# One ring for K, V and the weights: K and V of two kv heads per transfer, wo behind V

## The chip, the core and the metric

The kernel runs on one core of a Trainium2 chip. The metric is the time of one execution on the device in microseconds (us); the kernel before has a median of 214.87 us in 3 runs (214.87 to 214.9). Inputs and outputs lie in HBM.

## What is computed

One decode step for 4 sequences of one token each, with attention over the last 2,048 positions of a cache beside an MLP of two layers. Cut to what matters:

```python
def _A_ref(x, k_cache, v_cache, wq, wo):         # x (4, 1, 576); caches (4, 16, 8192, 128)
    W = min(4096, max(256, Sk // 4))             # 2048
    q = (x @ wq).reshape(B, Sq, 32, 128).transpose(0, 2, 1, 3)
    k = jnp.repeat(k_cache[:, :, Sk - W:, :], 2, axis=1)
    v = jnp.repeat(v_cache[:, :, Sk - W:, :], 2, axis=1)
    p = softmax(jnp.einsum("bhqd,bhkd->bhqk", q, k) * (128 ** -0.5))
    o = jnp.einsum("bhqk,bhkd->bhqd", p, v)
    return o.transpose(0, 2, 1, 3).reshape(B, Sq, 4096) @ wo

def _B_ref(x, w1, w2, w3, w4):
    h = gelu(layernorm(x) @ w1)
    ...
    x1 = x + hs                                  # with one token, half of hs's input is zero
    return x1 + gelu(layernorm(x1) @ w3) @ w4    # w3 (576, 4608), w4 (4608, 576)

xn = layernorm(A_x)
out = A_x + _A_ref(xn, A_k_cache, A_v_cache, A_wq, A_wo) + _B_ref(xn, B_w1, B_w2, B_w3, B_w4)
```

Everything is bf16. K and V are 33.6 MB each, the weights together 21.4 MB; each byte is read once.

## The kernel before

**Order of work.** The author writes each engine's work as a list of operations with a key (lines 165 to 178). The list is sorted by key (line 577), and each engine runs its own in that order; an operation waits for the semaphores of those named in `waits` (line 593). All large transfers are issued by SP, one behind the other, into one queue: a transfer that has to wait for a buffer holds up those behind it in SP's list. PE's work on K and on V stands in two loops of NIT = 4 passes (lines 374 to 388 and 453 to 456), each pass of four kv heads; all else is unrolled.

**Transfers.** SP's list (lines 216 to 251) is: wq in two pieces of two rows per partition and a ragged part, w2, w1, w3 in two pieces and a ragged part, then K. A kv head of K, for all 4 sequences, is one transfer of 2,048 KB: partition 4i + b holds positions 64i to 64i + 63 of sequence b, one run of 16 KB (lines 231 to 233). K goes through a ring of NKS = 4 such slots of its own, V through another of NVS = 4. wq, w1 and w2 lie in V's ring before V, w3 in `regB`, which later holds the transposed K. V0 is issued after K8 (`V0_AFTER`), V1 to V3 after K15, then wo into K's ring (`WO_AFTER`), then V4 to V15, each when the PV of four heads before is done (line 241), and w4 in five pieces (`W4P`, line 248), each when the last PV over its place in V's ring is done.

**Head of the kernel.** Layer norms; q = xn @ wq (line 316); w2 and w1 (line 497); w3 as h2_0 to h2_4, 12 matmuls each (lines 518 to 533); gelu2 (line 535); zeroS, which clears the scores' PSUM banks (line 338).

**K.** For each group of 8 x 128 positions, T (line 352) is 8 transposes on PE with `perm_k` as the moving operand, into one of 4 PSUM buffers; the copy out of PSUM (lines 356 to 360) is done by ACT for groups 1, 4 and 7 of each 8 and by DVE for the others, into 16 places of `ktbuf`. SC (lines 362 to 372) makes one kv head's scores in 16 matmuls of 512 columns, four sequences side by side in four column groups of PE. It is issued two groups after the last group that it needs (line 385). POOL copies each head's queries into `Qs` (line 390).

**Softmax.** rmax over all scores (line 394), exp on ACT in four parts (line 399), a transpose of 32 x 32 blocks on DVE (line 402), a permutation matmul PTp (line 403) and a copy PTs out of PSUM (lines 407 and 410, two each on ACT and DVE). PTg (line 413) spreads a head's probabilities over 4 sequences with the mask `bmask`, zero where the partition holds another sequence.

**V.** PV (lines 445 to 456) is 64 matmuls per head with V as the stationary operand and 8 columns of PTg; DVE scales the result into `OTx` (line 457).

**Tail.** After the last PV: turn (line 472), ORT (line 478), AO = 64 matmuls with wo (lines 466 to 479), MO0 = w4's first piece in 28 matmuls of 288 columns over four column groups, a fold of the four sums into two (lines 546 to 556), and MO1 to MO4 for the other four pieces, 88 matmuls of 144 columns over two column groups (lines 558 to 570). Then DVE and ACT copy the sums out (lines 571 and 572), and two transfers store them.

Of the kernel before, what the change touches and what calls it, by code (L numbers as in the profile page):

```python
# [12 lines left out]
NKS = 4  # L13
NVS = 4
NPG = 4
NKT = 16
NTB = 4
NIT = 4
ACT_EVAC = (1, 4, 7)
WO_AFTER = 3  # L20
V0_AFTER = 8
# [17 lines left out]
def bass_parallel_sum__sliding_block_cached__mixer_s_mlp__decode_kernel(  # L39
# [9 lines left out]
    NT = W // 32  # L49
    UE = NT * 128  # L50
    NHB = 8 * G
# [10 lines left out]
    with ExitStack() as ctx:  # L62
# [10 lines left out]
        kring = kring_t[:].rearrange("p (s t d) -> p s t d", s=NKS, t=NT)  # L73
        vring = vring_t[:].rearrange("p (s t d) -> p s t d", s=NVS, t=NT)
        ktbuf = regB_t[:, 0:NKT * 1024].rearrange("p (s n) -> p s n", s=NKT)
        kttile = regB_t[:, 0:NKT * 1024].rearrange("p (t b i) -> p t b i", b=B, i=32)
        w3main = regB_t[:, 0:4 * F].rearrange("p (r n) -> p r n", r=4)
        w3rag = regB_t[:, 4 * F:W3E]
        wqmain = vring_t[:, 0:4 * Hq * Dh].rearrange("p (r n) -> p r n", r=4)
        wqrag = vring_t[:, 4 * Hq * Dh:4 * Hq * Dh + Hq * Dh // 2]  # L80
        wo_sb = kring_t[:, 0:32 * D].rearrange("p (r n) -> p r n", r=32)
        _o = 4 * Hq * Dh + Hq * Dh // 2
        w1p = vring_t[:, _o:_o + 9 * HALF]
        _o += 9 * HALF
        w2p = vring_t[:, _o:_o + 9 * HALF]
        _o += 9 * HALF
        WQ_SLOTS = -(-_o // UE)
        assert WQ_SLOTS < NVS

# [53 lines left out]
        OTps = lambda g: ps[:, 4 + g % 4, 0:8]  # L143
# [41 lines left out]
        KT = KV + G + 8.0  # L185
# [12 lines left out]
        P(lambda e: e.memset(Qs[:, 3], 0.0), sig=("qs", 3), key=-95.8)  # L198

        def first_counts(e):  # L200
            for k in range(NTB):
                e.sem_inc(S[("eb", 32 - NTB + k)], 1)
                e.sem_inc(S[("on", k)], 1)
        P(first_counts, key=-95.7)
        P(lambda e: e.tensor_copy(out=perm_k[:].rearrange("p (b i) -> p b i", b=B), in_=ident_bf[:].rearrange("p (i b) -> p b i", b=B)),
          waits=["ident_bf"], sig="perm_k", key=-95.5)
        P(lambda e: e.tensor_copy(out=perm_p[:].rearrange("p (i b) -> p i b", b=B), in_=ident_bf[:].rearrange("p (b i) -> p i b", b=B)),
          waits=["ident_bf"], sig="perm_p", key=-95)
# [22 lines left out]
        def kv_pairs(ring_t, slot, cache, g):  # L231
            return [(ring_t[:, slot * UE:(slot + 1) * UE],
                     cache[:, g, Sk - W:Sk, :].rearrange("b (i t) d -> i b (t d)", t=NT))]

        for g in range(G):
            ev_k.append(add_dma(kv_pairs(kring_t, g % NKS, A_k_cache, g), ("k", g % NKS),
                                [f"T{8 * (g - NKS) + 7}"] if g >= NKS else [], g))
        wo_wait = f"T{8 * (G - 2) + 7}"
        for g in range(G):
            kk = KS + g if g else V0_AFTER + 0.5  # L240
            w = [f"PV{g - NVS}"] if g >= NVS else (["hT"] if g < WQ_SLOTS else [])
            ev_v.append(add_dma(kv_pairs(vring_t, g % NVS, A_v_cache, g), ("v", g % NVS), w, kk))
            if g == WO_AFTER:
                ev_wo = add_dma([(kring_t[:, 0:32 * D], A_wo.rearrange("(p r) n -> p (r n)", r=32))],
                                "wo", [wo_wait], kk + 0.1)
        w4_src = B_w4.rearrange("(p r) n -> p r n", r=RT)
        w4_sb = vring_t[:, 0:RT * D].rearrange("p (t n) -> p t n", n=D)
        for n, (t0, t1_) in enumerate(W4P):
            lst = (t1_ * D - 1) // UE
            ev_w4.append(add_dma([(w4_sb[:, t0:t1_, :], w4_src[:, t0:t1_, :])], ("w4", n),  # L250
                                 [f"PV{max(g for g in range(G) if g % NVS == lst)}"], KS + G + 0.1 * n))
# [94 lines left out]
        def pe_T(n):  # L346
            g, k = n // 8, n % 8

            def f(e):
                ins = None  # L350
                for t in range(8):
                    ins = e.transpose(tb[n % NTB][:, t, :], kring[:, g % NKS, 8 * k + t, :], perm_k[:])  # L352
                return ins
            return f
# [7 lines left out]
        def pe_SC(g):  # L362
            def f(e):
                ins = None
                for c4 in range(4):
                    for b in range(B):
                        t0 = 8 * ((8 * g + 2 * c4) % NKT)
                        ins = e.matmul(Sps[32 * b:32 * b + 32, c4, :].rearrange("p (t i) -> p t i", t=16), lhsT=Qs[:, g % 4, b, :],  # L368
                                       rhs=kttile[:, t0:t0 + 16, b, :],
                                       start=False, stop=(g == G - 1), tile_position=(0, 32 * b), skip_group_check=True)  # L370
                return ins
            return f

        for n in range(NHB):
            p = n % 32
            w = [("L", ("k", p // 8), 16)] if p % 8 == 0 else []
            w.append(("L", ("eb", (p - NTB) % 32), 1))
            add("pe", pe_T(n), waits=w, sig=f"T{n}", key=n // 32 + 0.01 * p, loop=("k", n // 32))
            eng, f = evac(n)
            add(eng, f, waits=[f"T{n}"] + ([f"SC{n // 8 - 2}"] if n >= 8 else []), sig=("eb", p), key=n + 0.2)  # L380
        for g in range(-1, G):
            s_ = g % 4
            if g < G - 1:
                add("pe", pe_SC(g), waits=[("L", ("eb", 8 * s_ + 6), 1), ("L", ("eb", 8 * s_ + 7), 1), ("L", ("qs", s_), 1)], sig=f"SC{g}",
                    key=(g + 1) // 4 + 0.01 * (8 * ((g + 1) % 4) + 1) + 0.005, loop=("k", (g + 1) // 4))
            else:
                add("pe", pe_SC(g), waits=[("c", ("eb", 30), NIT + 1), ("c", ("eb", 31), NIT + 1), ("c", ("qs", 3), NIT + 1)],
                    sig=f"SC{g}", key=NIT + 0.5)
        for g in range(G):
            P(lambda e, g=g: e.tensor_copy(out=Qs[:, g % 4], in_=Qpad[:, g]), waits=(["qT"] if g == 0 else []) + ([f"SC{g - 4}"] if g >= 3 else []),  # L390
              sig=("qs", g % 4), key=8 * g)


        add("dve", lambda e: e.tensor_reduce(out=rmax[:], in_=Sps, axis=AX.XY, op=ALU.max), waits=[f"SC{G - 1}"], sig="rmax", key=KS)  # L394
        add("dve", lambda e: e.tensor_scalar(out=negb[:], in0=rmax[:], scalar1=-scale, scalar2=None, op0=ALU.mult),
            waits=["rmax"], sig="negb", key=KS + 0.05)
        for q in range(4):
# [5 lines left out]
            add("pe", lambda e, q=q, cs=cs: e.matmul(ps[:, q, :], lhsT=perm_p[:], rhs=PTb[:, cs], start=True, stop=True),  # L403
                waits=[f"PTb{q}"] + (["perm_p"] if q == 0 else []), sig=f"PTp{q}", key=KS + 0.2 + 0.01 * q)
            dst = PTs[:, 16 * q:16 * q + 16, :].rearrange("p t r -> p (t r)")
            if q % 2 == 1:
                add("act", lambda e, q=q, dst=dst: e.activation(out=dst, in_=ps[:, q, :], func=ACTF.Copy), waits=[f"PTp{q}"],
                    sig=f"PTs{q}", key=KS + 0.3 + 0.01 * q)
            else:
                add("dve", lambda e, q=q, dst=dst: e.tensor_copy(out=dst, in_=ps[:, q, :]), waits=[f"PTp{q}"],  # L410
                    sig=f"PTs{q}", key=KS + 0.3 + 0.01 * q)
        for g in range(G):
            add("dve", lambda e, g=g: e.tensor_tensor(  # L413
                out=PTg[:, g % NPG], in0=PTs[:, :, 2 * g:2 * g + 2].unsqueeze(2).to_broadcast([128, NT, B, 2]),
                in1=bmask[:].unsqueeze(1).to_broadcast([128, NT, B, 2]), op=ALU.mult),
                waits=[f"PTs{q}" for q in range(4)] + ["bmask"] if g < NPG else [f"PV{g - NPG}"], sig=("pg", g % NPG),
                key=KS + 0.4 + 0.01 * g if g < NPG else KV + g - NPG + 0.6)
# [241 lines left out]
```

## Time and profile before

| what | value |
|---|---|
| median of 3 runs | 214.87 us |
| the profiled execution | 214.88 us |
| its span, first to last instruction | 213.6 us |
| HBM read in the span | 88.49 MB, 414 GB/s |
| mean granted TensorE clock | 0.776 |
| 16 K transfers, 2,048 KB each | 15.7 us from issue to landing (median) |
| 16 V transfers, 2,048 KB each | 17.6 us |
| wo, 4,608 KB | 23.6 us |

The prediction shows lines of the profile. In the page, the first part has each engine's busy time, its share of the span and its instructions; PE is the matmuls, PEld the loads of the stationary operand. The second part cuts the span into 40 slices of 5.3 us; a digit is the busy share in tenths, for PEclk the granted clock of TensorE in tenths, for DMA the busy share of the 16 DMA engines. The time from issue to landing holds the wait behind earlier transfers in the queue. In the timeline, a row is start, duration, engine, line, operation, output<-input, shapes and count, and in brackets the idle time before it with what ended it.

### The profile page before, as it was taken

The page shows a single profiled execution, that of the slowest core. Times are in us where ns is not written, and L with a number is a line of the kernel's source. Part 1 is how long each engine was busy: PE and PEld are TensorE (multiplying, and loading weights), DVE is VectorE, ACT ScalarE, POOL GpSimd, SP SyncE. Part 2 cuts the span into 40 slices and gives each one's busy share as a digit, 9 for nine tenths or more (in the row PEclk, how much of TensorE's full clock was granted, in tenths as well). Part 3 has the DMA queues.
Part 4 walks back from the last instruction along what each step waited for, and adds up shares of the span by engine and source line. Part 5 has one row for each costly group of instructions (what it writes and reads, how often), then busy time and mean ns, then how long its engine had stood idle before and what let it go on. Part 6 is the DMA issues. An engine that isn't in the chain of part 4 may idle for free.

```text
span 213.6 us, 5830 instructions
## 1 busy us (share of the span) xinstructions
PE 138.9 (65%) x2692; PEld 108.9 (51%) x2692; DVE 87.3 (41%) x162; ACT 59.3 (28%) x72; POOL 12.0 (6%) x39
## 2 busy tenths in 40 slices
PE   0089347999999994999999729823343443333585
PEld 0036123777777883788887503823343443333444
DVE  6725202566666664366666569611111112100000
ACT  2000302466665553266566654000000000000000
POOL 8501000000000100000000000000000000000000
PEclk9999855899999999699999995555555555555579
DMA  6999999999999999999999999999999999999993
GB/s 243 426 404 446 438 412 439 423 422 417 436 426 420 426 439 429 417 433 431 429 417 439 429 429 441 427 417 426 420 433 433 426 420 436 433 417 429 432 408 125
DMA packets 6657, 88.63 MB, mean 415 GB/s; under 512 B 748, under 2 KB 888, under 8 KB 1656
## 3 DMA queue, kind: packets, MB, share of 16 engines
q1 hardware_dynamic: 6632, 88.50, 97.8%
q8 instruction: 7, 0.11, 0.2%
q14 instruction: 2, 0.02, 0.0%
q10 hardware_dynamic: 16, 0.01, 0.0%
HBM read 88.49 MB, written 0.00 MB: 414 GB/s over the span
## 4 chain that ended last, share of the span: by engine, by line
DMA 52%; PE 39%; DVE 4%; issue 2%; SPq 1%; ACT 1%
PE ps L352 23%; DMA vring<-in_A_v_cache_dram 23%; DMA regB<-in_B_w_dram 12%; DMA kring<-in_A_k_cache_dram 8%; DMA vring<-in_B_w_dram 8%; PE ps L368 7%; PE ps L449 4%; PE ps L544 1%; PE ps L528 1%; DVE PTb L402 1%; SPq L176 1%; DVE rmax L394 1%; PE ps L341 1%; DVE regB L360 1%; ACT PTb L538 1%
## 5 line engine op out<-in xcount | busy, mean ns | idle before, releaser
L360 DVE COPY regB<-ps 128x1024 bf16<-128x1024 bf16 x80 | 52.4, 687 | 34.1 <-PE ps L352 32.3
L352 PEld LDWEIGHTS ps<-perm_k,kring 128*128 128x128 bf16 x1024 | 59.2, 100 | 11.6 <-issue 8.2
L352 PE MATMUL ps<-perm_k,kring 128*128 128x128 bf16 x1024 | 62.4, 222 | 3.2 <-DMA kring<-in_A_k_cache_dram 3.1
L359 ACT ACTIVATE regB<-ps 128x1024 bf16<-128x1024 bf16 x48 | 47.7, 1023 | 40.9 <-PE ps L352 40.9
L449 PE MATMUL ps<-PTg,vring 128*128 128x8 bf16 x1024 | 29.5, 168 | 39.0 <-DMA vring<-in_A_v_cache_dram 36.4
L449 PEld LDWEIGHTS ps<-PTg,vring 128*128 128x128 bf16 x1024 | 28.4, 104 | 40.1 <-DMA vring<-in_A_v_cache_dram 27.5
L457 DVE TENSOR_TENSOR PTb<-ps,PTb 128x32 bf16<-128x32 f32 x16 | 3.1, 192 | 56.1 <-PE ps L449 56.1
L368 PE MATMUL ps<-regB,Qs 128*32 128x512 bf16 x272 | 18.7, 396 | 4.6 <-issue 3.5
L554 ACT ACTIVATE P_sb<-ps 100x288 f32<-100x288 f32 x1 | 0.4, 411 | 75.8 <-PE ps L464 75.8
L368 PEld LDWEIGHTS ps<-regB,Qs 128*32 128x32 bf16 x272 | 6.6, 97 | 10.8 <-issue 6.4
L413 DVE TENSOR_TENSOR PTg<-PTs,bmask 128x512 bf16<-128x512 bf16 x16 | 10.7, 682 | 0.0
L390 POOL COPY Qs<-Qpad 128x128 bf16<-128x128 bf16 x16 | 4.6, 296 | 91.3 <-PE ps L368 82.0
L528 PE MATMUL ps<-regB,x1nT 128*32 128x432 bf16 (+1 forms) x60 | 4.4, 459 | 6.0 <-DMA regB<-in_B_w_dram 6.0
L541 DVE STREAM_TRANSPOSE h2T_sb<-PTb 128x1152 bf16<-128x1152 bf16 x1 | 1.4, 1379 | 11.4 <-ACT PTb L538 11.4
L528 PEld LDWEIGHTS ps<-regB,x1nT 128*32 128x32 bf16 x60 | 1.8, 122 | 8.0 <-DMA regB<-in_B_w_dram 6.6
L403 PE MATMUL ps<-PTb,perm_p 128*128 128x512 bf16 x4 | 2.4, 607 | 4.3 <-DVE PTb L402 4.1
L294 PE MATMUL ps<-ident_bf,xn_bf 4*128 4x4 bf16 x4 | 0.3, 166 | 7.5 <-DVE ragsrc L278 7.5
L571 DVE CAST out_sb<-ps 36x144 bf16<-36x144 f32 x1 | 0.3, 301 | 9.9 <-PE ps L544 9.9
L464 PE MATMUL ps<-kring,ORT 128*4 128x288 bf16 x64 | 4.0, 441 | 0.4 <-DVE ORT L478 0.4
L294 PEld LDWEIGHTS ps<-ident_bf,xn_bf 4*128 4x128 bf16 x4 | 0.2, 110 | 7.4 <-POOL ones_f L213 7.4
L316 PE MATMUL ps<-vring,xnT 128*32 128x512 bf16 x40 | 3.9, 571 | 0.0
L403 PEld LDWEIGHTS ps<-PTb,perm_p 128*128 128x128 bf16 x4 | 0.4, 104 | 6.3 <-DVE PTb L402 6.3
(99 smaller groups left out, 79.1 us busy)
## 6 DMA issues: line engine op xcount, KB each, us to landing
kring<-in_A_k_cache_dram SPq DMA_DIRECT2D x16, 2048.0 KB, 15.7
vring<-in_A_v_cache_dram SPq DMA_DIRECT2D x16, 2048.0 KB, 17.6
regB<-in_B_w_dram SPq DMA_DIRECT2D x2, 2304.0 KB, 23.5
kring<-in_A_wo_dram SPq DMA_DIRECT2D x1, 4608.0 KB, 23.6
vring<-in_A_wq_dram SPq DMA_DIRECT2D x2, 2048.0 KB, 9.6
vring<-in_B_w_dram SPq DMA_DIRECT2D x2, 2016.0 KB, 17.4
vring<-in_B_w_dram SPq DMA_DIRECT2D x2, 648.0 KB, 14.3
vring<-in_B_w_dram SPq DMA_DIRECT2D x1, 720.0 KB, 14.4
```

What stands on the lines that cost most here:

```text
L316: ins = e.matmul(Qps[32 * j:32 * j + 32, k, :], lhsT=x_, rhs=w, start=(r == 0), stop=(r == 4), tile_position=(0, 32 * j))
L352: ins = e.transpose(tb[n % NTB][:, t, :], kring[:, g % NKS, 8 * k + t, :], perm_k[:])
L359: return "act", lambda e: e.activation(out=ktbuf[:, n % NKT], in_=src, func=ACTF.Copy)
L360: return "dve", lambda e: e.tensor_copy(out=ktbuf[:, n % NKT], in_=src)
L368: ins = e.matmul(Sps[32 * b:32 * b + 32, c4, :].rearrange("p (t i) -> p t i", t=16), lhsT=Qs[:, g % 4, b, :], rhs=kttile[:, t0:t0 + 16, b, :],
L390: P(lambda e, g=g: e.tensor_copy(out=Qs[:, g % 4], in_=Qpad[:, g]), waits=(["qT"] if g == 0 else []) + ([f"SC{g - 4}"] if g >= 3 else []), ...
L403: add("pe", lambda e, q=q, cs=cs: e.matmul(ps[:, q, :], lhsT=perm_p[:], rhs=PTb[:, cs], start=True, stop=True), waits=[f"PTb{q}"] + (["per ...
L413: add("dve", lambda e, g=g: e.tensor_tensor(out=PTg[:, g % NPG], in0=PTs[:, :, 2 * g:2 * g + 2].unsqueeze(2).to_broadcast([128, NT, B, 2]) ...
L449: ins = e.matmul(OTps(g), lhsT=vring[:, g % NVS, t, :], rhs=PTg[:, g % NPG, t].rearrange("p b e -> p (b e)"), start=(t == 0), stop=(t == N ...
L457: add("dve", lambda e, g=g: e.tensor_tensor(out=OTx[:, :, 2 * g:2 * g + 2, :], in0=OTps(g).rearrange("p (b e) -> p b e", b=B).unsqueeze(3) ...
L464: return e.matmul(ACC[h], lhsT=lhsT, rhs=rhs, start=start, stop=stop, tile_position=(k0, 32 * h))
L528: ins = e.matmul(H2ps[k][32 * j:32 * j + 32, :], lhsT=x_, rhs=w, start=(r == 0), stop=(r == 4), tile_position=(0, 32 * j))
```

## The change

K and V are cut into 8 units of two kv heads (u and u + 8), 4,096 KB each; partition 8i + m holds positions 128i to 128i + 127 of the m-th of 8 pairs of sequence and head, one run of 32 KB. One ring of NSL = 4 such slots replaces both rings. The weights of the head lie in slots 1 to 3, so K0 goes to slot 0 at once, and K1 to K3 wait for h2_4, the last matmul with w3. w3 without its ragged part is one transfer. V0 to V3 each wait for the transposes of the unit of K that had the slot, V4 to V7 for the PV of four units before; wo waits for PV6 and stands behind V7, w4 behind wo without waits of its own. PE's loops have 2 passes, each of four units. SC is made in 32 pieces of 8 matmuls, each over four groups T. PTp has two permutations per part, so 8 matmuls and 8 copies PTs (4 on DVE, 4 on ACT). PTg is two operations per unit, each of 1,024 elements per partition, with a bf16 mask, in NPG = 2 buffers; PV is 128 matmuls of 16 columns per unit.

```diff
-NKS = 4
-NVS = 4
-NPG = 4
+NSL = 4
+NPG = 2
-NIT = 4
+NIT = 2
-WO_AFTER = 3
-V0_AFTER = 8
...
+    NU = G // 2
-    NT = W // 32
+    NT = W // 16
     UE = NT * 128
-    NHB = 8 * G
+    NB = NT // 8
+    NHB = NB * NU
...
-        kring_t = sb("kring", [128, NKS * UE], BF16)
-        vring_t = sb("vring", [128, NVS * UE], BF16)
-        W3E = 4 * F + FH
-        regB_t = sb("regB", [128, max(NKT * 1024, W3E)], BF16)
+        ring_t = sb("ring", [128, NSL * UE], BF16)
+        regB_t = sb("regB", [128, NKT * 1024], BF16)
...
-        for r in (0, 2):
-            ev_w3 += 2 * [add_dma([(w3main[:, r:r + 2, :], w3_src[:, r:r + 2, :])], ("w3", r), (), -12 + r)]
+        ev_w3 += 4 * [add_dma([(w3main, w3_src)], ("w3", 0), (), -12)]
...
+        def kv_pairs(slot, cache, u):
+            heads = cache.rearrange("b g s d -> (b g) s d")[u:B * G:NU, Sk - W:Sk, :]
+            return [(ring_t[:, slot * UE:(slot + 1) * UE], heads.rearrange("m (i t) d -> i m (t d)", t=NT))]
+
+        def k_done(u):
+            return f"T{NB * u + NB - 1}"
+        for u in range(NU):
+            w = [k_done(u - NSL)] if u >= NSL else (["h2_4"] if u else [])
+            ev_k.append(add_dma(kv_pairs(u % NSL, A_k_cache, u), ("k", u % NSL), w, u))
+        for u in range(NU):
+            w = [f"PV{u - NSL}"] if u >= NSL else [k_done(NU - NSL + u)]
+            ev_v.append(add_dma(kv_pairs(u % NSL, A_v_cache, u), ("v", u % NSL), w, KS + u))
+        ev_wo = add_dma([(wo_sb, A_wo.rearrange("(p r) n -> p r n", r=32))], "wo", [f"PV{NU - NSL + OUT_SLOT}"], KS + NU)
         w4_src = B_w4.rearrange("(p r) n -> p r n", r=RT)
         for n, (t0, t1_) in enumerate(W4P):
-            lst = (t1_ * D - 1) // UE
             ev_w4.append(add_dma([(w4_sb[:, t0:t1_, :], w4_src[:, t0:t1_, :])], ("w4", n),
-                                 [f"PV{max(g for g in range(G) if g % NVS == lst)}"], KS + G + 0.1 * n))
+                                 (), KS + NU + 0.1 * (n + 1)))
...
+        def pe_SC(c):
+            u, c4 = c // 4, c % 4
             def f(e):
                 ins = None
-                for c4 in range(4):
+                t0 = 8 * ((4 * c) % NKT)
+                for h in range(2):
                     for b in range(B):
-                        t0 = 8 * ((8 * g + 2 * c4) % NKT)
...
+                        ins = e.matmul(Sps[32 * b:32 * b + 32, c4, :].rearrange("p (t i) -> p t i", t=32), lhsT=Qs[:, 2 * (u % NSL) + h, b, :],
+                                       rhs=kttile[:, t0:t0 + 32, 2 * b + h, :],
+                                       start=False, stop=(u == NU - 1), tile_position=(0, 32 * b), skip_group_check=True)
...
+        for c in range(NHB // 4):
+            q = c % NQ
...
+            add("pe", pe_SC(c), waits=w, sig=f"SC{c}", key=c // NQ + 0.01 * (4 * q + 5) + 0.005, loop=("k", c // NQ))
...
+            def fan(e, j=j):
+                ins = None
+                for h in range(2):
+                    r = 2 * (j + NU * h)
+                    ins = e.tensor_tensor(out=PTg[:, j % NPG, :, :, 2 * h:2 * h + 2], in0=PTs[:, :, r:r + 2].unsqueeze(2).to_broadcast([128, NT, B, 2]),
+                                          in1=bmask[:, h].unsqueeze(1).to_broadcast([128, NT, B, 2]), op=ALU.mult)
+                return ins
...
                 for t in range(NT):
-                    ins = e.matmul(OTps(g), lhsT=vring[:, g % NVS, t, :], rhs=PTg[:, g % NPG, t].rearrange("p b e -> p (b e)"),
+                    ins = e.matmul(OTps(j), lhsT=ring[:, j % NSL, t, :], rhs=PTg[:, j % NPG, t].rearrange("p b e -> p (b e)"),
                                    start=(t == 0), stop=(t == NT - 1))
```

More of the change, by code (lines that the diff above doesn't have):

```diff
@@ L395, in bass_parallel_sum__sliding_block_cached__mixer_s_mlp__decode_kernel @@
+        for u in range(NU):
+            for h in range(2):
+                P(lambda e, u=u, h=h: e.tensor_copy(out=Qs[:, 2 * (u % NSL) + h], in_=Qpad[:, u + NU * h]),
+                  waits=(["qT"] if u + h == 0 else []) + ([f"SC{4 * (u - NSL) + 3}"] if u >= NSL else []),
+                  sig=("qs", 2 * (u % NSL) + h), key=u + 0.1 * h)
+        add("dve", lambda e: e.tensor_reduce(out=rmax[:], in_=Sps, axis=AX.XY, op=ALU.max), waits=[f"SC{NHB // 4 - 1}"], sig="rmax", key=KS)
         add("dve", lambda e: e.tensor_scalar(out=negb[:], in0=rmax[:], scalar1=-scale, scalar2=None, op0=ALU.mult),
```

188 lines of the change are left out of this document (89 added, 99 removed).

## Prediction

> **What bounds the kernel now.** I read the page first: the busy share of each engine, the DMA line in 40 slices, the clock line and the share of the DMA queue.
>
> ```profile
> PE 138.9 (65%) x2692; PEld 108.9 (51%) x2692; DVE 87.3 (41%) x162; ACT 59.3 (28%) x72; POOL 12.0 (6%) x39
> PEclk9999855899999999699999995555555555555579
> DMA  6999999999999999999999999999999999999993
> q1 hardware_dynamic: 6632, 88.50, 97.8%
> ```
>
> No engine is near its limit, and the transfers are: the queue that SP feeds takes 97.8% of 16 engines' span for 88.50 MB, and no slice but the first and the last is below 9. The change moves the same bytes. So the whole of its gain must lie in the rate while the queue is full, and it can lose in three ways: the queue runs dry, or the head or the tail grows, in which the queue is not the limit. For the rate I asked for windows in which runs of one size prevail (columns: stretch, length, busy time of PE, PEld, DVE, ACT, POOL, granted clock, DMA share, GB/s).
>
> ```profile
> 0.00:1.80 1.80, 0.00 (x0) 0.00 (x0) 0.00 (x0) 0.39 (x1) 1.13 (x8) 1.00 0.00 1
> 4.00:12.00 8.00, 1.04 (x20) 0.73 (x24) 6.10 (x18) 0.40 (x2) 4.08 (x13) 1.00 1.01 432
> 13.40:16.00 2.60, 2.17 (x28) 0.64 (x20) 0.38 (x1) 0.38 (x1) 0.00 (x0) 1.00 1.02 421
> 18.00:27.00 9.00, 5.24 (x60) 3.07 (x57) 3.49 (x11) 2.18 (x4) 0.42 (x2) 0.90 1.01 432
> 146.00:198.00 52.00, 19.81 (x684) 18.93 (x681) 6.89 (x19) 0.00 (x0) 0.00 (x0) 0.50 1.01 428
> ```
>
> wq in 16 KB runs goes at 432 GB/s, w2 and w1 in 5,184 B runs at 421, w3 in 18 KB runs at 432, V in 16 KB runs at 428. The end of the span I read from the chain (start, length, what) and from PE's timeline.
>
> ```profile
> 191.08 17.48 DMA vring<-in_B_w_dram
> 208.60 3.17 PE ps L544 x88
> 211.79 0.30 DVE out_sb L571
> ...
> 198.97 1.87 PE L449 MATMUL ps<-PTg,vring 128*128 128x8 bf16 x64 [3.03 <-DMA vring<-in_A_v_cache_dram]
> 201.97 4.01 PE L464 MATMUL ps<-kring,ORT 128*4 128x288 bf16 x64 [0.38 <-DVE ORT L478]
> 205.77 1.17 PE L464 MATMUL ps<-vring,h2T_sb 128*4 128x288 bf16 x28
> 207.46 0.66 PE L544 MATMUL ps<-P_sb,sel_h 100*4 100x144 f32 x8 [0.52 <-ACT P_sb L554]
> 208.60 3.15 PE L544 MATMUL ps<-vring,h2T_sb 128*4 128x144 bf16 x88 [0.48 <-DMA vring<-in_B_w_dram]
> ```
>
> The last V lands at 198.97 and its work ends at 200.84; AO (64 matmuls) follows at 201.97, MO0 (28) directly behind it, the fold, and at 208.60, when w4's second piece has landed, the 88 matmuls of MO1 to MO4. They follow w4's small pieces to the end.
>
> **The change, part by part.** The sum is made on the profiled execution, 214.88 us (span 213.6 and 1.3 around it); the median is 214.87, the same.
>
> *Longer runs.* 16 engines move a 16 KB run in 16 x 16,384 B / 432 GB/s = 607 ns each and a 5,184 B run in 16 x 5,184 / 421 = 197 ns: 410 ns for 11,200 B, which leaves 7 ns per run whatever its size. K and V are 4,096 runs now, 256 per engine; as 2,048 runs, 128 per engine are saved: 128 x 7 = 0.9 us. Bounds: w3's 18 KB runs are no faster than wq's 16 KB runs (both 432), so the gain may be 0.2; and if the two-head pattern brought K and V from 428 to wq's 432, 67.1 MB would save 1.5 us. I take 0.9, which is nearest to the rows of single sizes. Half as many K and V transfers and w3 in one are 17 transfers fewer in a queue that is never empty; nothing.
>
> *K1 behind h2_4.* Slots 1 to 3 hold the weights, so K1 to K3 wait on SP for the last matmul with w3, and V0 and all else queues behind them.
>
> ```profile
> 29.81 3.07 PE L528 MATMUL ps<-regB,x1nT 128*32 128x432 bf16 x36 [4.19 <-DMA regB<-in_B_w_dram]
> 34.24 1.89 PE L341 MATMUL ps<-zeros_bf 128*128 128x512 bf16 x4 [1.36 <-ACT PTb L538]
> 36.22 1.03 PE L352 MATMUL ps<-perm_k,kring 128*128 128x128 bf16 x8
> ```
>
> w3's second half lands at 29.8. In one transfer all of it lands then, and 60 matmuls instead of 36 follow: 3.07 x 60/36 = 5.1, so h2_4 ends at 34.9. From issue to first bytes it is 1.0 (SP's first issue stands at 0.80, and the window to 1.80 has no traffic): K1 moves from 35.9. The cover is K0 behind w3's ragged part, 4.78 MB at 428 = 11.2 us, to 41.0. Cost nothing, 5 us in hand; without K0 there it would cost those 6 us.
>
> *K on PE.* PE starts when all of K0 is there, 41.0 instead of 36.2.
>
> ```profile
> 44.43 3.71 PE ps L352 x64
> 48.13 0.24 issue
> 48.37 1.05 PE ps L368 x16
> ```
>
> A kv head takes 3.71 + 0.24 + 1.05 = 5.0 us: 64 transposes, a wait for the copy out of PSUM (SC follows the last copy that it needs by two groups, before and after) and 16 score matmuls. The change has the same matmuls, in SCs of 8, twice as often. So there is one more wait of up to 0.24 per head and one more start and drain of a group, which no row shows by itself: 0.1 to 0.5 more by an estimate from these rows; I take 0.35, the wait and 0.1: 5.35 per head, 10.7 per unit, against 9.8 for its transfer. Were 32 B pieces of the moving operand slower than 64 B ones, it would be more. K ends at 41.0 + 8 x 10.7 = 126.6, and up to 3.4 later, as PE waits for K0 from about 38 and may begin at half clock: about 128.5, rmax at 130 instead of 123.9.
>
> *V4 behind PV0* is what this delay can reach: one ring has V0 to V3 in its slots, and V4 may go when PV0 is done.
>
> ```profile
> 123.90 2.29 DVE L394 TENSOR_REDUCE rmax<-ps 128x1 f32<-128x2048 f32 x1 [1.82 <-PE ps L368]
> 129.87 1.25 DVE L410 CAST PTs<-ps 128x512 bf16<-128x512 f32 x2
> 131.62 2.49 DVE L413 TENSOR_TENSOR PTg<-PTs,bmask 128x512 bf16<-128x512 bf16 x4
> 132.36 3.80 PE L449 MATMUL ps<-PTg,vring 128*128 128x8 bf16 x136
> ```
>
> From rmax to the first PV matmul it is 8.5 us. Added: two casts more on DVE, 1.25, and a first PTg of two operations of 1,024 elements instead of one of 512 at 0.62: between 1.25 (bf16 mask, twice the rate) and 2.5, so 0.6 to 1.9 more. PV0 is 128 matmuls at 28 ns, 3.6. It ends at 130 + 8.5 + 1.9 to 3.1 + 3.6 = 144 to 145.2. The queue holds work until K0's 41.0 and eleven units of 9.8, less 0.7 of the gain: 148.1; V4 must be issued by 147. Cost nothing, with 2 to 3 us in hand, the thinnest cover. Later releases have more: wo waits for PV6, done 4 us after V6's landing, while V7 moves for 9.7.
>
> *wo behind V.* The bytes up to w4 are the same, so w4's second piece lands at 208.6 - 0.9 = 207.7. But AO now waits for wo instead of the last V. wo ends where the last V ended, at 198.97 - 0.9 = 198.1, V7's work being over by 193. AO runs 198.1 to 202.1; MO0 waits for w4's first piece, one 2,016 KB transfer (4.8 us) before the second, 202.9; the fold is done at 206; MO1 starts at 207.7. The chain AO, MO0, fold, which was one stretch, is now three with pauses. That bears on the clock:
>
> ```profile
> 120.00:124.00 4.00, 2.70 (x46) 1.86 (x43) 2.13 (x5) 3.32 (x3) 0.00 (x0) 1.00 1.03 438
> 124.00:128.00 4.00, 0.00 (x1) 0.01 (x1) 3.12 (x4) 1.59 (x6) 0.00 (x0) 0.94 1.01 429
> 128.00:132.00 4.00, 3.75 (x9) 0.75 (x10) 3.93 (x9) 2.40 (x6) 0.00 (x0) 0.50 1.06 459
> ...
> 202.65:206.05 3.40, 3.40 (x64) 2.01 (x60) 0.00 (x0) 0.00 (x0) 0.00 (x0) 0.50 0.98 417
> 206.05:208.60 2.55, 1.55 (x37) 0.73 (x29) 0.00 (x0) 0.41 (x1) 0.00 (x0) 1.00 0.97 395
> 208.60:211.75 3.15, 3.15 (x88) 2.61 (x88) 0.00 (x0) 0.00 (x0) 0.00 (x0) 1.00 0.44 167
> ```
>
> The granted clock is 0.50 through V, rose only at 206.05, after 4.1 us of unbroken matmuls, and had fallen by 128 after 4 us of idleness. Now AO alone is 4.0 us, then come 0.8 of idleness, MO0, the fold, 1.7 of idleness. I expect no rise that lasts to MO1. At full clock its matmuls take 144 columns in two column groups, 30 ns apiece (88 in 3.15 us with small waits); at half clock 60. 88 x 60 = 5.3 us from 207.7, and 0.2 for the last one to drain: 213.2 instead of 211.8. **+1.4 us**, the gain of 0.9 already in it.
>
> [...]
>
> Sum: 214.88 + 1.4 = 216.3 us.
>
> **The rivals.** *The tail keeps its clock* (faster). A rise within AO that outlives the two pauses: MO4 then ends behind w4's last bytes as now, and 0.9 is gained: 214.0. For it: AO is only 0.1 us shorter than the stretch that raised it. Against: the pauses, 2.5 us of six. With a gain of 0.2 it would be no change, 214.7. It decides from a clock of 1.00 at MO1's start.
>
> *V4 comes too late.* If K on PE is 3 us slower than reckoned (half clock at its start, more waits), the cover is used up, and every us beyond empties the queue and moves the tail: 1 to 3 us on top, 217.5 to 219.
>
> *PE's code is loaded again.* The K loop's body doubles, from 320 matmuls to 640 with their weight loads.
>
> ```profile
> 58.36 1.05 PE L368 MATMUL ps<-regB,Qs 128*32 128x512 bf16 x16 [0.27 <-issue]
> q8 instruction: 7, 0.11, 0.2%
> ```
>
> Now the second pass begins (about 58) with a pause of 0.27, like any other, so nothing is loaded again; seven fetches of 16 KB serve the whole run, each 0.002 x 16 x 213.6 / 7 = 1.0 us. If the longer body no longer stays, a fetch with its delay of 1.0 stalls PE about 2 to 3 us on the one return, all of the cover and perhaps 1 us more: 217.3. [...]
>
> *The change doesn't do what it says:* longer runs move at the old rate, gain 0.2, and the cold tail stands: 217.0.
>
> **How the numbers follow.** Chances: forecast 0.50 (its own range 215.4 to 216.9, from gains of 1.5 and 0.2), tail at full clock 0.20, V4 late 0.16, code 0.05, no faster runs 0.09. Likeliest: 216.3. The range takes in the full-clock tail at 214.0 and the late V4 to 218.6. A measurement here can tell about 0.2%, 0.43 us, from no change. Faster than that is the tail at full clock with most of the gain, 0.14; within it the same with little gain, or a gain of 1.5 with the clock rising midway, 0.11; slower the rest, 0.75.
>
> **What would show it.** Right: DMA share 9 in all slices; V at 430 to 431 GB/s; AO starting at about 198; a clock of 0.50 at MO1's start and some 5 us for the 88. Wrong: a clock of 1.00 there; a dip of DMA near 148 (V4) or 41 (K1); rmax later than 133; V at 428 or below, as then the two-head pattern costs rather than gains.

## The result and the profile after

The kernel after the change takes 376.56 us (median of 6 runs, 374.11 to 378.4), the kernel before 214.87 us in the runs beside it: a ratio of 1.752 (95% interval 1.744 to 1.759). The forecast of 216.3 us, its range and every rival are far off. The profiled execution took 377.55 us with a span of 376.3.

The page of the kernel after: the DMA lines of the 40 slices (9.4 us each now), then the share of the queue and the transfers of K and V.

```profile
DMA  8999999999999999999999999999999999999993
GB/s 323 446 404 256 223 195 197 224 214 218 202 211 219 218 219 216 219 220 216 216 212 216 216 214 212 214 212 211 202 218 216 212 206 206 216 212 214 412 420 132
...
q1 hardware_dynamic: 4184, 88.49, 97.9%
...
ring<-in_A_k_cache_dram SPq DMA_DIRECT2D x8, 4096.0 KB, 64.5
ring<-in_A_v_cache_dram SPq DMA_DIRECT2D x8, 4096.0 KB, 69.7
```

Read the DMA line alone, and nothing seems wrong: the engines are as busy as before, 97.9% for the same 88.49 MB. The line under it tells the story: K begins within the fourth slice (256 GB/s), and from the fifth to the last of V the same full engines move 195 to 224 GB/s; in the full slices of weights ahead of K and behind V they move 404 to 446. So no wait took the place of another. By these rates each packet takes twice as long (worked out below). The windows of the kernel after show that the rate belongs to K and V alone (columns as in the prediction):

```profile
4.00:12.00 8.00, 1.16 (x24) 0.83 (x28) 5.98 (x18) 0.41 (x2) 4.72 (x15) 1.00 1.01 430
...
60.00:180.00 120.00, 74.35 (x979) 57.11 (x979) 40.93 (x61) 37.09 (x37) 2.14 (x8) 0.76 1.00 215
210.00:340.00 130.00, 28.00 (x905) 25.18 (x903) 14.57 (x38) 1.22 (x3) 0.00 (x0) 0.50 1.00 211
360.00:365.00 5.00, 4.29 (x84) 2.46 (x80) 0.00 (x0) 0.00 (x0) 0.00 (x0) 0.65 1.00 423
```

V went at 428 GB/s before and goes at 211 now. With all 16 engines busy and 213 GB/s, between K's 215 and V's 211, a run of 32 KB takes 16 x 32,768 B / 213 GB/s = 2.46 us, where 1.22 would fit the rate before. A unit of 4,096 KB lands every 19.7 us instead of 2 x 4.9 = 9.8, and 16 x (19.7 - 9.8) = 158 us is nearly all of the 162 us by which the kernel is slower. The rest of the timeline of the kernel after, before K and after V, looks as it was forecast:

```profile
29.85 4.99 PE L548 MATMUL ps<-ring,x1nT 128*32 128x432 bf16 x60 [7.16 <-DMA ring<-in_B_w_dram]
34.88 1.82 SPq L180 DMA_DIRECT2D ring<-in_A_k_cache_dram  x3
...
359.58 4.01 PE L484 MATMUL ps<-ring,ORT 128*4 128x288 bf16 x64 [6.34 <-DMA ring<-in_A_wo_dram]
364.30 1.03 PE L484 MATMUL ps<-ring,h2T_sb 128*4 128x288 bf16 x28 [0.71 <-DMA ring<-in_B_w_dram]
...
369.44 4.98 PE L564 MATMUL ps<-ring,h2T_sb 128*4 128x144 bf16 x88 [2.93 <-DMA ring<-in_B_w_dram]
```

K1 is issued at 34.88; AO, MO0 and MO1 each wait for their weights with pauses between, and the 88 matmuls take 4.98 us.

### The profile page after: what moved, and what is told of

It reads as the page before. It is cut to its first block, busy times and chain, and to the rows that moved or that the text cites. A ratio compares the mean times of both kernels' runs of the same rounds, so it can differ in the third digit from the quotient of the medians.

```text
span 376.3 us, 5772 instructions
## 1 busy us (share of the span) xinstructions
PE 158.0 (42%) x2678; PEld 120.2 (32%) x2680; DVE 89.7 (24%) x164; ACT 61.0 (16%) x74; POOL 12.1 (3%) x41
## 3 DMA queue, kind: packets, MB, share of 16 engines
q1 hardware_dynamic: 4184, 88.49, 97.9%
HBM read 88.49 MB, written 0.00 MB: 235 GB/s over the span
## 4 chain that ended last, share of the span: by engine, by line
another core or an unknown queue 35%; PE 30%; DMA 27%; ACT 3%; DVE 3%; issue 1%; SPq 1%; DVEq 0%
DMA ring<-in_B_w_dram 17%; PE ps L356 16%; DMA ring<-in_A_k_cache_dram 10%; PE ps L464 7%; PE ps L374 5%; ACT regB L363 2%; PE ps L548 1%; PE ps L564 1%; SPq L180 1%; DVE PTb L408 1%; DVE PTs L419 1%; DVE rmax L400 1%; DVE PTg L426 0%; ACT P_sb L405 0%
## 5 line engine op out<-in xcount | busy, mean ns | idle before, releaser
L356 PE MATMUL ps<-perm_k,ring 128*128 128x128 bf16 x1024 | 77.2, 243 | 63.5 <-DMA ring<-in_A_k_cache_dram 63.5
L356 PEld LDWEIGHTS ps<-perm_k,ring 128*128 128x128 bf16 x1024 | 70.1, 111 | 81.1 <-DMA ring<-in_A_k_cache_dram 45.2
L464 PE MATMUL ps<-PTg,ring 128*128 128x16 bf16 x1024 | 28.6, 174 | 110.5 <-DMA ring<-in_A_v_cache_dram 110.1
L464 PEld LDWEIGHTS ps<-PTg,ring 128*128 128x128 bf16 x1024 | 27.9, 104 | 111.4 <-DMA ring<-in_A_v_cache_dram 94.2
L426 DVE TENSOR_TENSOR PTg<-PTs,bmask 128x1024 bf16<-128x1024 bf16 x16 | 10.2, 684 | 0.0
L548 PE MATMUL ps<-ring,x1nT 128*32 128x432 bf16 (+1 forms) x60 | 5.0, 525 | 7.2 <-DMA ring<-in_B_w_dram 7.2
L484 PE MATMUL ps<-ring,ORT 128*4 128x288 bf16 x64 | 4.0, 443 | 6.3 <-DMA ring<-in_A_wo_dram 6.3
L564 PE MATMUL ps<-ring,h2T_sb 128*4 128x144 bf16 x88 | 5.0, 307 | 2.9 <-DMA ring<-in_B_w_dram 2.9
L564 PEld LDWEIGHTS ps<-ring,h2T_sb 128*4 128x4 bf16 x88 | 4.8, 120 | 3.2 <-DMA ring<-in_B_w_dram 3.2
L320 PE MATMUL ps<-ring,xnT 128*32 128x512 bf16 x40 | 4.2, 607 | 0.0
```

The source lines that it names most:

```text
L320: ins = e.matmul(Qps[32 * j:32 * j + 32, k, :], lhsT=x_, rhs=w, start=(r == 0), stop=(r == 4), tile_position=(0, 32 * j))
L356: ins = e.transpose(tb[n % NTB][:, t, :], ring[:, u % NSL, 8 * k + t, :], perm_k[:])
L426: ins = e.tensor_tensor(out=PTg[:, j % NPG, :, :, 2 * h:2 * h + 2], in0=PTs[:, :, r:r + 2].unsqueeze(2).to_broadcast([128, NT, B, 2]), in1 ...
L464: ins = e.matmul(OTps(j), lhsT=ring[:, j % NSL, t, :], rhs=PTg[:, j % NPG, t].rearrange("p b e -> p (b e)"), start=(t == 0), stop=(t == NT ...
L484: return e.matmul(ACC[h], lhsT=lhsT, rhs=rhs, start=start, stop=stop, tile_position=(k0, 32 * h))
L548: ins = e.matmul(H2ps[k][32 * j:32 * j + 32, :], lhsT=x_, rhs=w, start=(r == 0), stop=(r == 4), tile_position=(0, 32 * j))
```

## The experiments

Three things are new in how K and V are read: the run is 32 KB, the eight pairs of one unit lie further apart in HBM than four sequences did, and the source's slowest dimension has 16 blocks (with 8 pairs each) where it had 32 (with 4 sequences each). **My theory after the result:** it is the split. By this theory a transfer is shared out over the 16 DMA engines by the slowest dimension, so that one engine gets whole blocks; the number of busy engines in e2 agrees (DMA share 0.50 with 8 blocks, 0.25 with 4, 0.13 with 2). With 16 x 8 each engine then has one block of 8 partitions, which I take to be 8e to 8e + 7 for engine e; with 32 x 4 it has two blocks of 4 partitions. Which engine has which block no trace here shows. Engines that run abreast may then hold each other up, depending on the partitions that they write; this was my estimate, and the runs below test it. **Rivals:** the distances in HBM; the length of the run.

**Transfers alone, one shape after the other (e1_streams).** A kernel without any computing reads eight streams of 16.8 MB. The shapes, as (count, stride) from slow to fast:

```python
("A", 8192, [(8192, 32), (16 * HEAD, 4)])      # 32 x 4, 16 KB runs: the kernel before
("B", RUN, [(RUN, 16), (8 * HEAD, 8)])         # 16 x 8, 32 KB runs: the kernel after
("C", 8192, [(RUN, 16), (8 * HEAD, 8)])        # 16 x 8, 16 KB runs
("D", RUN, [(RUN, 32), (16 * HEAD, 4)])        # 32 x 4, 32 KB runs
("E", RUN, [(RUN, 128)])                       # 128 x 1, contiguous
("G", RUN, [(RUN, 16), (HEAD, 8)])             # 16 x 8, pairs 2 MB apart
("H", RUN, [(RUN, 16), (16 * RUN, 8)])         # 16 x 8, contiguous
("I", RUN, [(RUN, 16), (8 * HEAD + 2048, 8)])  # 16 x 8, pairs 16 MB + 4 KB apart
```

> Only transfers, no arithmetic: the kernel leaves out the whole computation and stores zeros. Eight stages of 16.8 MB each, SP waiting for all transfers between them. A: the pattern of before (32 positions blocks x 4 sequences, 16 KB runs). B: the changed pattern (16 blocks x 8 heads that lie 16 MB apart, 32 KB runs). C: as B with 16 KB runs, twice as many transfers. D: 32 blocks x 4 sequences with 32 KB runs. E: 128 runs of 32 KB from one contiguous 4 MB. G: as B with 8 adjacent heads, 2 MB apart. H: 16 blocks x 8, but all from one contiguous 4 MB (8 parts 512 KB apart). I: as B with the heads 16 MB + 4 KB apart. All theories expect A at 428 GB/s (39 us) and B at 214 (78 us). Theory of the distance (streams that move at the same time read places a large power of two apart and share a part of HBM): C 214, D, E and H 428, I 428, G open. Rival, the run length (32 KB itself is slow): C 428, D, E, G, H and I 214. Rival, the split (a source of 16 x 8 runs is spread badly over the 16 engines): C, G, H and I 214, D and E 428.

The windows of this run, one in each stream (columns: stretch, length, busy time of DVE and POOL, granted clock, DMA share, GB/s):

```profile
3.00:40.00 37.00, 0.00 (x0) 0.00 (x0) 1.00 1.01 429
48.00:120.00 72.00, 0.00 (x0) 0.00 (x0) 1.00 1.01 211
130.00:200.00 70.00, 0.00 (x0) 0.00 (x0) 1.00 1.00 213
210.00:245.00 35.00, 0.00 (x0) 0.00 (x0) 1.00 0.98 425
252.00:287.00 35.00, 0.00 (x0) 0.00 (x0) 1.00 1.01 434
295.00:368.00 73.00, 0.00 (x0) 0.00 (x0) 1.00 1.00 208
378.00:450.00 72.00, 0.00 (x0) 0.00 (x0) 1.00 1.01 211
460.00:533.00 73.00, 0.00 (x0) 0.00 (x0) 1.00 1.00 208
```

A, D and E go at the full rate, the five streams of 16 x 8 at half of it. B and C differ in the run alone and are equal, as are A and D: run length falls. H reads one contiguous stretch and is as slow as B, and D, with sequences 32 MB apart, has the full rate: distance falls. What is common to the slow ones is 16 blocks of 8.

**How the rate falls with the split (e2_splits).** Again transfers alone, all contiguous, 32 KB runs: 64 x 2, 32 x 4, 16 x 8, 8 x 16, 4 x 32, 2 x 64 on 128 partitions, then two shapes on 64 partitions and one on 32, whose transfers go by turns to the lower and the upper half of SBUF.

```python
("8x16", RUN, [(2 * n * HEAD, [(RUN, 8), (8 * RUN, 16)]) for n in range(2)])
("64 of 64", 64, [(n * HEAD, [(RUN, 64)]) for n in range(4)])
("64 as 16x4", 64, [(n * HEAD, [(RUN, 16), (16 * RUN, 4)]) for n in range(4)])
```

> Only transfers, no arithmetic; zeros are stored. Nine stages, SP waiting between them, all from contiguous places, all in 32 KB runs, only the shape of the source differs: 128 partitions as 64x2 and 32x4 (four transfers of 4.2 MB each), 16x8 and 8x16 (two each), 4x32 and 2x64 (one each); then 64 partitions as 64 and as 16x4 and 32 partitions as 32, four transfers each, by turns in the lower and the upper half of SBUF. [...] Rival, the number of the slowest dimension alone (16 or fewer is slow for a reason on the side of the read): 64 partitions as 64 at 428, as 16x4 at 214.

Its windows, one per shape in that order (the last two columns are the ones to read):

```profile
1.00:39.00 38.00, 0.14 (x1) 0.00 (x0) 1.00 0.97 414
42.50:81.00 38.50, 0.00 (x0) 0.00 (x0) 1.00 0.98 420
84.50:124.00 39.50, 0.00 (x0) 0.00 (x0) 1.00 1.01 212
127.50:204.00 76.50, 0.00 (x0) 0.00 (x0) 1.00 0.50 110
207.00:283.00 76.00, 0.00 (x0) 0.00 (x0) 1.00 0.25 55
285.00:363.00 78.00, 0.00 (x0) 0.00 (x0) 1.00 0.13 54
365.00:405.00 40.00, 0.00 (x0) 0.00 (x0) 1.00 1.01 210
408.00:448.00 40.00, 0.00 (x0) 0.00 (x0) 1.00 0.99 210
450.50:471.00 20.50, 0.00 (x0) 0.00 (x0) 1.00 0.96 205
```

The DMA share counts engines: 0.50 is 8 of 16, 0.25 is 4, 0.13 is 2. So the slowest dimension does set how many engines work. Divide the rate by them: 26 GB/s per engine in the first two shapes, 13 to 14 in the next three, and with 2 x 64 again 27. The two engines of 2 x 64 begin at partitions 0 and 64 and don't disturb each other (27 GB/s each); the four of 4 x 32 begin at 0, 32, 64 and 96 and do (14 each). My reading is that engines 32 partitions apart hold each other up and engines 64 apart don't. With 16 x 8, the blocks that begin at partitions 8e and 8(e + 4) are 32 apart: by this reading each engine has one partner, and each gets half (13 GB/s). In 64 x 2 and 32 x 4 (26 each), engines with partitions 32 apart would then not write them at the same moment; how those blocks are shared out isn't shown.

64 partitions give half in either shape, also as 64 blocks of one run, where a rule that only counts the blocks (16 or fewer are slow) would have had 428; so the loss has to do with where the runs go in SBUF. 32 partitions are as fast as 64, 205 against 210.

Transfers to 64 partitions keep 16 engines busy (shares of 1.01 and 0.99) at 13 GB/s each, those to 32 partitions (0.96) too. Which engine writes which partition, and what it is that engines 32 partitions apart would share, no trace here shows; the pairing is inferred from the shares and rates.

**The kernel before with this split alone (f2_before_16x8).** Ring, order, loops and run length are those of the kernel before. Only each K and V transfer is taken as 16 blocks of 8 heads (its compute then works on differently placed data):

```diff
+            heads = cache.rearrange("b g s d -> (b g) s d")[g // 2:B * G:8, Sk - W:Sk, :]
...
-                      cache[:, g, Sk - W:Sk, :].rearrange("b (i t) d -> i b (t d)", t=NT))]
+                      heads.rearrange("m (i z t) d -> z i m (t d)", z=2, t=NT)[g % 2])]
```

> The kernel before whole, with 16 KB runs, its own two rings and order; only the source of K and V is taken as 16 blocks x 8 heads instead of 32 blocks x 4 sequences, so partitions get other positions than its arithmetic supposes (all of K and V are read, once). Theory (the split alone does it): 67.1 MB at 214 instead of 428 GB/s, 157 us more: 365 to 375 us. Rival (it takes 32 KB runs or the one ring as well): 215 us.

It takes 368.2 us in its one run. Its windows in K and V:

```profile
60.00:160.00 100.00, 56.75 (x744) 43.51 (x748) 30.75 (x47) 28.85 (x29) 2.66 (x9) 0.83 1.01 219
180.00:330.00 150.00, 43.91 (x1062) 36.37 (x1060) 28.71 (x55) 13.46 (x19) 0.00 (x0) 0.57 1.01 233
```

The second window has 233 because it also holds wo, whose fullest slice of the page has 381 GB/s; V by itself is slower, 214 to 223 in its slices. The split alone suffices: 153 of the 162 us, with nothing else of the change. (The eight sources of a transfer lie 16 MB apart here, four sequences lay 32 MB apart; e1 showed that distance doesn't matter.)

**The change without this split (f1_after_contig).** The kernel after, whole, but a unit is read as 128 contiguous runs of 32 KB (other positions of the caches, as many bytes):

```diff
-            heads = cache.rearrange("b g s d -> (b g) s d")[u:B * G:NU, Sk - W:Sk, :]
-            return [(ring_t[:, slot * UE:(slot + 1) * UE], heads.rearrange("m (i t) d -> i m (t d)", t=NT))]
+            n = 128 * UE
+            flat = cache.rearrange("b g s d -> (b g s d)")[u * n:(u + 1) * n]
+            return [(ring_t[:, slot * UE:(slot + 1) * UE], flat.rearrange("(p e) -> p e", p=128))]
```

> The changed kernel whole, but K and V are read from contiguous 4 MB pieces of the caches as 128 runs of 32 KB, so other positions are used than the reference's; everything else (one ring, 32 KB runs, two-head units, wo behind V, w3 in one) stays. Theory (the split of the 16x8 source is the whole of the loss, and the rest is as predicted): 216.3 us, 215.4 to 216.9, with half clock in the tail. Rival (the ring of four units or the longer K on PE lose as well): 220 or more, with the queue empty before V4.

216.9 us, 1.0112 times before (1.0081 to 1.0143); the profiled run has 216.36. This is the kernel that I had forecast at 216.3. Its windows in K, around V4, in V, and from the fold into the 88 matmuls (columns as in the prediction):

```profile
52.00:100.00 48.00, 43.97 (x708) 34.00 (x705) 29.03 (x45) 25.73 (x26) 2.12 (x8) 1.00 1.02 435
144.00:147.00 3.00, 1.48 (x56) 1.38 (x52) 1.49 (x4) 0.00 (x0) 0.00 (x0) 0.50 0.96 355
147.00:149.00 2.00, 0.86 (x32) 0.87 (x33) 0.00 (x0) 0.00 (x0) 0.00 (x0) 0.50 0.90 377
150.00:180.00 30.00, 16.99 (x614) 16.58 (x610) 7.44 (x20) 0.00 (x0) 0.00 (x0) 0.50 1.00 430
...
206.10:208.70 2.60, 0.00 (x2) 0.01 (x2) 0.00 (x0) 0.00 (x0) 0.00 (x0) 1.00 0.94 386
208.70:210.00 1.30, 1.30 (x37) 1.30 (x39) 0.00 (x0) 0.00 (x0) 0.00 (x0) 0.85 0.47 183
210.00:211.00 1.00, 1.00 (x22) 1.00 (x20) 0.00 (x0) 0.00 (x0) 0.00 (x0) 0.50 0.30 107
```

Units land 9.71 us apart; two V transfers of one head each take 9.79 in the kernel before. But V4, issued at 144.87, lands at 158.61, 10.81 behind V3 (147.80), and the rate dips to 355 and 377 between. Rows of its timeline, rmax on DVE and then PE:

```profile
131.01 2.29 DVE L401 TENSOR_REDUCE rmax<-ps 128x1 f32<-128x2048 f32 x1 [1.59 <-PE ps L375]
```

```profile
199.10 3.92 PE L485 MATMUL ps<-ring,ORT 128*4 128x288 bf16 x64 [6.58 <-DMA ring<-in_A_wo_dram]
203.82 1.03 PE L485 MATMUL ps<-ring,h2T_sb 128*4 128x288 bf16 x28 [0.80 <-DMA ring<-in_B_w_dram]
...
208.70 4.55 PE L565 MATMUL ps<-ring,h2T_sb 128*4 128x144 bf16 x88 [2.67 <-DMA ring<-in_B_w_dram]
```

The profiled run is 1.48 us slower than the one of the kernel before, and 1.40 of it stands in these 88 matmuls, 4.55 us against 3.15. The clock was not at half when they began: it rose at the end of AO, was 1.00 until 208.70, fell about 0.9 us into them (0.85 in the mean to 210.00) and was 0.50 in the window behind.

**Moving the engines apart (e3_offset, e4_offset, e5_leads).** If two engines 4 apart hold each other up because they run in step, then making one lag by half a unit should help, with the shape unchanged. Transfers alone: units of 16 x 8, first plain, then behind two short lead transfers, one of 12 blocks and one of 4. By the shares of e2 they occupy 12 and 4 engines; that these are engines 0 to 11 and 0 to 3, so that in each pair one engine starts later, is supposed. e3 leads with 12 x 4 and 4 x 4 runs (and has a third part, in which SP reads the lower and ACT the upper 64 partitions), e4 with 12 x 2 and 4 x 4 (a lag of 2 runs for half of the pairs, of 4 for the others), e5 with 12 x 5 and 4 x 5, then 12 x 6 and 4 x 6, then 12 x 5 alone.

```python
load(sp, lead_t[0:12 * r, :], 0, [(RUN, 12), (12 * RUN, r)], s_lead)
if both:
    load(sp, lead2_t[0:4 * r, :], 0, [(RUN, 4), (4 * RUN, r)], s_lead2)
stream(8)      # eight units of [(RUN, 16), (16 * RUN, 8)]
```

> Only transfers, no arithmetic; zeros are stored. First stage: four transfers of 4.2 MB as 16x8 in 32 KB runs, as the changed kernel has them. [...] Third stage: 16.8 MB as transfers of 16x4 runs, SP loading the lower 64 partitions and ACT the upper 64 at the same time. [...]

e3's windows: plain, behind the leads, two queues.

```profile
3.00:80.00 77.00, 0.00 (x0) 0.00 (x0) 1.00 1.01 210
120.00:200.00 80.00, 0.00 (x0) 0.00 (x0) 1.00 0.99 326
215.00:280.00 65.00, 0.00 (x0) 0.00 (x0) 1.00 1.02 218
```

> Transfers alone, nothing computed (zeros are stored, and the positions read are other ones): four units of 4,096 KB as 16 blocks x 8 heads, then a lead of 12 x 2 runs and one of 4 x 4 runs of 32 KB, then eight units more of the same shape. [...] Rival (a shift helps by some fixed part only, since the shape itself is slow): they stay at 12.75 us (329 GB/s), as in the run with one longer lead, or go back to 20.

e4's windows: plain, behind the shorter lead.

```profile
2.00:80.00 78.00, 0.00 (x0) 0.00 (x0) 1.00 1.02 213
110.00:200.00 90.00, 0.00 (x0) 0.00 (x0) 1.00 1.00 239
```

> Transfers alone, nothing computed (zeros are stored, and the positions read are other ones): eight units of 4,096 KB as 16 blocks x 8 heads behind leads of r runs of 32 KB for each of engines 0 to 11 and again r for each of engines 0 to 3, with r = 5, then r = 6, then with the first lead alone (r = 5). [...] Rival (a lead of any kind loosens the shape): with the first lead alone it is as fast as with both; or the three do not follow r, and stay at 12 to 18 us.

e5's windows: r = 5, r = 6, and r = 5 with the first lead alone.

```profile
45.00:110.00 65.00, 0.00 (x0) 0.00 (x0) 1.00 1.00 341
175.00:265.00 90.00, 0.00 (x0) 0.00 (x0) 1.00 1.00 257
320.00:445.00 125.00, 0.00 (x0) 0.00 (x0) 1.00 0.99 213
```

The same transfers, of the same shape, go at 210 GB/s or at up to 341, by nothing but what stood ahead of them in the queue. The state lasts for all eight units. A unit takes 20 us plain, 17.3 behind e4's 2 and 4 runs, 12.75 behind 4, 12.4 behind 5, 16.3 behind 6; with the second lead missing, so that engines 0 to 3 would start with their partners, it is 19.7, as if there were no lead. So most of the loss comes from how the engines run beside each other, and not from the shape or the bytes by themselves. Misses: I had expected full rate in e3 and e4, and 10.5 us for r = 5 with a gentle fall at 6. The rate does turn back past some 4 to 5 runs (341 GB/s at 5, 257 at 6), as a lag of half a unit, 4 runs of 8, would make it, but it peaks near 340 GB/s and falls faster than my estimate from one lag per pair. Why the best lag doesn't give 428 stays open. Two queues with 64 partitions each don't help, 218.

**The clock in the tail (f3_keep_clock).** f1 with 20 matmuls of zeros ahead of AO and 10 ahead of MO1, which keep PE busy:

```diff
+        add("pe", pe_keep(20), waits=["turn"], sig="keep0", key=KV + 19.95)
...
+        add("pe", pe_keep(10), waits=[], sig="keep1", key=KT + 20.6)
```

> f1_after_contig (the changed kernel with K and V from contiguous places, so other positions than the reference's) with 20 more matmuls of zeros into a free PSUM bank between the last PV and AO and 10 more between the fold and MO1. If the tail of f1 is slow by the clock, these keep it up: AO, MO0 and MO1 at a granted clock of 1.00, the 88 matmuls in about 3.2 us instead of 4.6, and 215.2 us (1.4 less than f1's profiled 216.4; the runs of f1 go from 216.4 to 218.0). Rival (the tail follows w4's pieces or the order of the work, not the clock): 216.4 to 217 as in f1.

216.78 us, 1.0097 times before (1.0066 to 1.0128); the profiled run has 215.12. PE's timeline at its end:

```profile
199.28 2.14 PE L485 MATMUL ps<-ring,ORT 128*4 128x288 bf16 x64 [0.26 <-DMA ring<-in_A_wo_dram]
...
208.91 3.09 PE L574 MATMUL ps<-ring,h2T_sb 128*4 128x144 bf16 x88 [0.43 <-DMA ring<-in_B_w_dram]
```

With the zeros AO takes 2.14 us instead of 3.92, and MO1 to MO4 take 3.09 instead of 4.55, near the 3.15 that they took at a clock of 1.00 in the kernel before: 1.46 us of the profiled run is the tail's clock. The median doesn't follow, since its runs spread from 215.12 to 217.4, and the slower ones have the lower mean clock, 0.803 against 0.832. Why they do isn't shown. The gain is shown for the profiled run, not for the median.

**V4 earlier (f4_later_sc).** f3 with SC one group later, so that PE has no wait for the last copy out of PSUM:

```diff
-            add("pe", pe_SC(c), waits=w, sig=f"SC{c}", key=c // NQ + 0.01 * (4 * q + 5) + 0.005, loop=("k", c // NQ))
+            add("pe", pe_SC(c), waits=w, sig=f"SC{c}", key=c // NQ + 0.01 * (4 * q + 6) + 0.005, loop=("k", c // NQ))
```

> The changed kernel with K and V read as contiguous 4,096 KB (other positions of the caches) and the zero matmuls ahead of AO and MO1 that keep the clock, and SC one group later, so that PE has no wait for the last copy out of PSUM. Theory (V4's late issue at 144.9 costs 1.1 us, as the fastest DMA engines have run dry 2.4 us before the slowest): rmax 1.5 to 2.5 us earlier than 131.0, V4 issued at 142.5 to 143.5, V4 lands 9.7 to 9.9 us after V3 instead of 10.8, and the profiled time is about 214.0, against 215.1 with SC where it was. Rival (what follows V4 is late for another reason): V4's landing or the end doesn't move, 215.1 or more.

216.76 us, 1.0098 times before (1.0066 to 1.0131); 215.93 in the profiled run. Its timeline, DVE and PE:

```profile
123.58 2.29 DVE L401 TENSOR_REDUCE rmax<-ps 128x1 f32<-128x2048 f32 x1 [2.09 <-PE ps L375]
```

```profile
203.88 1.03 PE L485 MATMUL ps<-ring,h2T_sb 128*4 128x288 bf16 x28 [2.58 <-DMA ring<-in_B_w_dram]
...
206.89 3.08 PE L504 MATMUL ps<-zeros_bf 128*128 128x512 bf16 x9 [0.33 <-issue]
209.90 2.92 PE L574 MATMUL ps<-ring,h2T_sb 128*4 128x144 bf16 x88
```

K is done 7.4 us earlier (I had said 2), and V4 is issued at 137.44, 10 us ahead of V3's end. Yet V4 lands at 159.12, 11.2 behind V3, and V3 to V5 together take 20.8 us as in f1 and f3, where two units elsewhere take 19.4. **So my theory of V4's cover falls:** its late issue makes the dip, but V4 and V5 are 1.4 us late without it too. What makes them late is open. The first engine to finish V4 does so 9.69 us after the first to finish V3, on pace; the last is 11.20 behind the last. So one or two engines fall behind, not the queue as a whole, and the landing at 159.12 is that of the last engine. A candidate is PE's code: the instruction queue fetches 16 KB of it four times between 137 and 167 us in f1, f3 and f4; each fetch keeps one engine for 1.0 to 1.1 us, and the run behind it takes 1.7 us instead of 1.2. Against it: four fetches between 47 and 83 us move no unit of K by more than 0.3 us. No run without the fetches was made.

In this run the zero matmuls ran at half clock for the most part (0.68 in the mean over the nine, which took 3.08 us; 2.11 in f3) and ended only at 209.97, so that MO1 began 1.06 us after its data: the remedy cost what it should have saved.

No way was found to read the reference's positions in 32 KB runs at full rate with units of eight whole pairs of sequence and head: a head's 2,048 positions are 16 such runs, so the pairs stand as a second dimension behind 16 blocks. Other cuts, such as the 64 x 2 that went at 414 in e2, were not tried, and leads were not tried in the whole kernel; their best unit, 12.4 us, is longer than 9.8. No version that was run beat the kernel before.

## Why the prediction was wrong

- **What bounds the kernel:** right and of no use. The queue is the limit, 97.9%, with the same bytes; but I took the rate of a full queue as settled.
- **Longer runs:** this step failed. I put a gain of 0.9 us on it, with 0.2 and 1.5 as bounds, all from the length of the run. The rows behind them (wq, w3, V) are of transfers with 128 rows or 32 x 4; the new source has 16 blocks of 8, and no row of the trace has such a transfer. So the transfer was one that the trace doesn't show, and its price should have had a bound on the side of a loss as well. I did not look at the order of the source's dimensions at all; the closing sentence on V "at 428 or below" gave the two-head pattern no size. The runs showed some 158 us lost in its place: 211 to 215 GB/s instead of 428 (the profile after), by the 16 x 8 split alone (e1, e2, f2), and 216.9 us in all without that split (f1). What I did say of the length is near: in f1 the units come 0.08 us faster, 1.1 us over some 14 of them, against 0.9.
- **K1 behind h2_4:** 34.88 issued, 34.9 forecast, no cost.
- **K on PE:** f1 issues V0 to V3 10.74 us apart, 10.7 forecast; rmax at 131.0 instead of 130. One term was off: the SC of a pass's last four groups stands right behind them, not two groups later, and PE waits 1.21 us there for ACT's copy in f1, so that from K7's issue to V0's it is 11.69.
- **V4 behind PV0:** the fan (PTg) has the upper speed, 16 operations of some 0.68 us for 1,024 elements, against 0.68 for 512 before; V4 was issued at 144.87 in f1, within 144 to 145.2. That the cover costs nothing was wrong: the first engine is done with V3 at 145.96 and the last at 147.80, 1.84 us apart (2.4 in f4's expectation), so engines that are ahead run dry, and the rate falls from about 146, some 2 us ahead of V3's landing. And 1.4 us go at V4 and V5 for another reason (f4), which eat up the gain of the longer runs.
- **wo behind V:** right in the order and the pauses, half wrong in the clock. In f1 AO, MO0 and MO1 start at 199.1, 203.8 and 208.7, each 0.9 to 1.0 later than forecast, as the gain is gone by then. The clock did rise at the end of AO and lasted to MO1's start, 1.00, which the forecast had named as a sign of being wrong; it fell within MO1, and the 88 matmuls took 4.55 us, 5.3 forecast. In the kernel after it also rose at the end of AO, was 0.50 again before MO1, and they took 4.98. f3 shows that the clock makes the difference. That f1's profiled run has 216.36 against the forecast 216.3 is in part luck: MO1 began 1.0 later and took 0.8 less.
- **The sum's own bounds:** gains of 1.5 and 0.2 give 215.7 to 217.0, not 215.4 to 216.9. The chance of 0.20 for a tail at full clock was an estimate, and no run shows how often AO alone lifts the clock; in both profiled runs in which AO is work of 4 us on its own, f1 (3.92) and the kernel after (4.01), the clock rises at its end.
- **The rivals:** V4 too late is in part what f1 did (216.9 against 217.5 to 219). Code loaded again did not touch the K loop: no code is fetched between 83.7 and 145.7 us in f1, and the pause at the return is the wait for ACT's copy. In the first pass of V PE pauses for 2.66 and 3.72 us without any wait that the profile shows, each time around a code fetch. No rival had a slower transfer, though a full queue that moves the same bytes was all that the time depended on.

## What to carry to other kernels

Where a queue is full, first write down for each changed transfer how many blocks its slowest dimension has and which partitions each block fills, and compare it with a transfer in the trace of the same split, not of the same size. Here sources of 32, 64 and 128 blocks for 128 partitions went at 414 to 434 GB/s and 16 blocks of 8 at half of that. A DMA share of 1.00 isn't a rate: read the GB/s line beneath it.

## What had not been expected of the hardware

- Engines that hold one another up count as busy: the share is 1.01 at 211 GB/s and at 434 (e1).
- What a lead of some 4 runs changes lasts for eight units, 12.75 instead of 20 us each (e3); without the second lead all is as slow as before, 213 GB/s (e5).
- SC one group later takes the K loop from 10.74 to 9.75 us per unit (f4): 1.0 per unit, where I had expected some 2 over all eight.
